# Decode attention on one core: output projections with every fourth column of wo stationary, stored four neighbours to a partition

## The chip, the core and the metric

The kernel runs on one core of a Trainium2 chip. The metric is the device time of one execution in microseconds (us), the median of several runs; lower is better. One execution was also recorded by the hardware profiler; all views of the profile come from that one, and their times count from the first instruction of its span.

The engines go by the profile's names: PE is TensorE's matmul, PEld its load of the stationary operand (LDWEIGHTS), DVE is VectorE, ACT ScalarE, POOL GpSimd, SP SyncE. A name with a q (SPq, ACTq) is the sequencer that issues DMAs. L349 is line 349 of the kernel.

## The reference

Two attention blocks, A and B, each for one new token: a query projection, 32 heads of 128 against a cache of 16384 positions (B uses only the last 4096), a softmax, the weighted sum of V, and an output projection with `wo` of 4096 x 512. The two rows of 512 are put side by side.

```python
q = (x @ wq).reshape(B, Sq, Hq, Dh).transpose(0, 2, 1, 3)
scores = jnp.einsum("bhqd,bhkd->bhqk", q, k) * (Dh ** -0.5)
p = softmax(scores, axis=-1)
o = jnp.einsum("bhqk,bhkd->bhqd", p, v)
return o.transpose(0, 2, 1, 3).reshape(B, Sq, Hq * Dh) @ wo      # a, and b with k, v cut to the window
...
return jnp.concatenate([a, b], axis=-1)                           # (1, 1, 1024) bfloat16
```

## The kernel before

All of the K and V that is needed, 336 MB, passes through SBUF once. A step of A takes two heads, a step of B eight, in two halves `u`; there are 20 steps, and their order (`steps`) is written out, with B at steps 0, 7, 13 and 19. The kernel runs under a manual schedule: each engine does its instructions in the order in which the code issues them.

For each half, VectorE multiplies K by the query (`scores_prod`, L194), adds up in a tree (`scores_tree`, L201 and L207), and ScalarE does the exponentials. TensorE then forms the weighted sums of V (`pv`, L279), with 8 or 16 rows of probabilities stationary and V moving. `evict` and `columns` (L295, L310, L314) turn the sums into columns of `s.O`, 128 dims on the partitions, one column for each head. The L310 matmuls are in f32, with 128 columns of 8 or 16 rows stationary.

Loads of K, V, wq and wo are all issued from SP's queue. x is loaded, and A's output stored, from ACT's queue. The rings `kring` and `vring` have two slots each. A's wo takes half of the last K slot, and B's last V the other half; B's wo takes a V slot when the last `pv` has read it, in five pieces (`wo_pieces`, 16, 8, 4, 2 and 2 of the 32 rows of a partition).

The last step is B's. Its two halves don't go through `pv`, but through `pv_columns` (L321): 128 pairs of a weight load of V (128 x 128 bf16) and a matmul with 4 moving columns, which give columns of O at once. The tail, in the order of the code and so of TensorE:

- the last `pv` of A, then `pv_columns` of B's first half, and A's `columns`;
- for A: `permute_o` (a transpose L331, a copy L333, four matmuls L336, a cast L340) gives `s.Op`, whose partition p and column r belong to row 32p + r of wo; `project_out_columns` (L349); `store_out`;
- `pv_columns` of B's second half, then `permute_o`, `project_out_columns` and `store_out` for B.

`project_out_columns` makes the 512 outputs as four columns of 128. For each column `c`, it goes through the rows r of wo that a partition holds, with 128 neighbouring columns of wo stationary and one column of `s.Op` moving, 128 pairs in all for A. B does so for each of its five pieces, each into four columns of its own in PSUM, since the pieces land one after the other; these are added up at the end.

`store_out` copies the four columns to SBUF (for A on ScalarE, L365; for B the sum over the pieces on VectorE, L361), in f32. Output f = 128c + p then lies on partition p in column c. A transpose on TensorE (L367) makes four rows of 128 of it, a cast to bf16 (L374 or L371) brings them back to SBUF, and a DMA stores four rows of 256 bytes (L375 from ACT's queue, L372 from SP's). The tiles `cols` and `rows` have one buffer each, which A and B share.

Of the kernel before, what the change touches and what calls it, by code (L numbers as in the profile page):

```python
# [9 lines left out]
F32 = mybir.dt.float32  # L10
BF16 = mybir.dt.bfloat16
P = 128
ACT = mybir.ActivationFunctionType
ALU = mybir.AluOpType
AX = mybir.AxisListType
# [10 lines left out]
def kernel(  # L26
# [14 lines left out]
    nc = tc.nc  # L41
# [4 lines left out]
    DN = A_wo.shape[1]  # L46
# [8 lines left out]
    one = ctx.enter_context(tc.tile_pool(name="one", bufs=1))  # L55
    ps_t = ctx.enter_context(tc.tile_pool(name="ps_t", bufs=2, space=bass.MemoryType.PSUM))
# [10 lines left out]
    identf = singles.tile([P, P], F32, tag="identf")  # L67
# [5 lines left out]
    A, B = _Side(), _Side()  # L73
# [267 lines left out]

    def project_out_columns(s, pieces):
        nf, npc = DN // P, len(pieces)
        ps = ps_s.tile([P, npc, nf], F32, tag="sp", name="out_cols")
        r0 = 0
        for k, n in enumerate(pieces):
            for c in range(nf):
                for r in range(r0, r0 + n):
                    nc.tensor.matmul(  # L349
                        ps[:, k, c : c + 1], lhsT=s.wo_t[:, r, c * P : (c + 1) * P], rhs=s.Op[:, r : r + 1],  # L350
                        start=(r == r0), stop=(r == r0 + n - 1),
                    )
            r0 += n
        s.out_ps = ps

    def store_out(s):
        nf = DN // P
        f0 = 0 if s is A else DN
        cols = one.tile([P, nf], F32, tag="cols", name="cols")
        if s is B:  # L360
            nc.vector.tensor_reduce(  # L361
                out=cols[:, :], in_=s.out_ps[:, :, :].rearrange("p k c -> p c k"), axis=AX.X, op=ALU.add
            )
        else:
            nc.scalar.copy(cols[:, :], s.out_ps[:, 0, :])  # L365
        pr = ps_t.tile([nf, P], F32, tag="tp", name="out_rows")
        nc.tensor.transpose(pr[:, :], cols[:, :], identf[:, :])  # L367
        rows = one.tile([nf, P], BF16, tag="rows", name="rows")
        dst = out[0, 0, f0 : f0 + DN].rearrange("(c f) -> c f", c=nf)
        if s is B:  # L370
            nc.vector.tensor_copy(rows[:, :], pr[:, :])  # L371
            nc.sync.dma_start(out=dst, in_=rows[:, :])  # L372
        else:
            nc.scalar.copy(rows[:, :], pr[:, :])  # L374
            nc.scalar.dma_start(out=dst, in_=rows[:, :])  # L375

    wo_pieces = (16, 8, 4, 2, 2)
    with tc.manual_schedule():
# [65 lines left out]
        columns()  # L444
        permute_o(A)
        project_out_columns(A, (HQ,))
        store_out(A)
        pv_columns(NT - 1, 1)
        permute_o(B)
        project_out_columns(B, wo_pieces)  # L450
        store_out(B)


# [28 lines left out]
```

## Time and profile before

| | us |
|---|---|
| median of 3 runs (829.58 to 830.49) | 830.06 |
| the profiled execution | 829.86 |
| its span, first to last instruction | 828.1 |
| VectorE busy (92% of the span) | 761.4 |
| TensorE busy, matmul (47%) | 387.3 |
| L201, the tree, 160 instructions | 344.9 |
| L194, the product for A, 32 instructions | 277.5 |
| L349, 256 pairs, in two bursts: from 808.43 for 3.72 us and from 819.80, in two parts, to 824.71 | 7.3 of weight loads |
| end of VectorE's last step on K (L207) | 791.39 |
| bytes read from HBM | 352.32 MB, 425 GB/s |

The page of a profile gives the busy time of each engine, then a chain: from the last instruction it is followed back to what released it, or to the instruction before it on its engine. "issue" in it is time in which an engine waited for nothing that the profile shows. A group's line gives engine, line, operation, output and input, and counts; a weight load shows in PEld, and the matmul that uses it in PE. The end of a matmul is modelled, and matmuls are pipelined, so that the distance between starts says more than the duration.

A line of the timeline has the start in us, the length, the engine, the line, the operation and the tiles; in brackets what its engine waited for before. The windows view gives for a stretch the busy time and number of instructions of each engine, the share of its full clock that TensorE was granted, and what the DMA engines did.

### The profile page before, as it was taken

Reading aid. Unit: us, or ns where it says so; the run is one execution under the profiler, and the core shown is the slowest. Engines: PE = TensorE matmul, PEld = TensorE weight load, DVE = VectorE, ACT = ScalarE, POOL = GpSimd, SP = SyncE. Lnnn points to the kernel's source line nnn. Section 1 sums busy time; section 2 is a strip of 40 time slices with the busy share of each in tenths; the row PEclk is TensorE's granted clock in tenths of the full one; section 3 lists DMA queues with packets and bytes.
Section 4 is the critical chain, followed back from the end, with each engine's and each line's share of the span. In section 5 each row is a group of like instructions: output and inputs, shape, how many; then the busy total and the mean of one; then the engine's idle time right before and its main releaser. Section 6 shows DMA issues by size and latency. Waiting matters only on the chain.

```text
span 828.1 us, 4994 instructions
## 1 busy us (share of the span) xinstructions
PE 387.3 (47%) x2100; PEld 171.3 (21%) x2100; DVE 761.4 (92%) x357; ACT 67.2 (8%) x195; POOL 0.7 (0%) x6
## 2 busy tenths in 40 slices
PE   3505061807173544637080826445362718081776
PEld 1201020303031212213030302122121203030335
DVE  1899999999999999999999999999999999999920
ACT  0111010101000001101010000011010101010110
POOL 0000000000000000000000000000000000000000
PEclk9766576859585868677685859586767767585975
DMA  9999999999999999999999999999999999999995
GB/s 380 431 431 431 428 453 423 449 416 436 431 427 431 431 440 423 439 423 455 412 450 416 452 412 432 442 423 445 419 443 418 441 421 444 424 432 432 430 430 240
DMA packets 10694, 352.64 MB, mean 426 GB/s; under 512 B 1456, under 2 KB 1456, under 8 KB 1840
## 3 DMA queue, kind: packets, MB, share of 16 engines
q1 hardware_dynamic: 10376, 352.33, 98.8%
q8 instruction: 16, 0.26, 0.1%
q10 hardware_dynamic: 296, 0.00, 0.0%
q14 instruction: 6, 0.05, 0.0%
HBM read 352.32 MB, written 0.00 MB: 425 GB/s over the span
## 4 chain that ended last, share of the span: by engine, by line
DVE 80%; DMA 15%; PE 3%; issue 1%; SPq 0%; ACT 0%; DVEq 0%
DVE kt L201 36%; DVE kt L194 36%; DMA kt<-in_A_k_cache_dram 10%; DVE sc L207 5%; DMA kt<-in_B_k_cache_dram 5%; PE o L279 1%; PE out_cols L349 1%; DVE m L212 1%; PE ocol L321 1%; DVE Mr L223 1%; DVE M L219 1%; DVE r L267 0%; SPq L135 0%; PE oc L310 0%; PE out_rows L367 0%
## 5 line engine op out<-in xcount | busy, mean ns | idle before, releaser
L201 DVE TENSOR_TENSOR kt<-kt 128x8192 bf16<-128x8192 bf16 (+3 forms) x160 | 344.9, 2156 | 4.7
L279 PE MATMUL o<-vt,pm 128*8 128x512 bf16 (+1 forms) x1216 | 306.7, 419 | 1.2 <-DMA vt<-in_A_v_cache_dram 1.2
L194 DVE TENSOR_TENSOR kt<-kt,qA 128x16384 bf16<-128x16384 bf16 x32 | 277.5, 8673 | 3.1 <-DMA kt<-in_A_k_cache_dram 3.1
L279 PEld LDWEIGHTS <-pm 128*8 128x8 bf16 (+1 forms) x1216 | 112.8, 94 | 185.4 <-issue 60.6
L214 PE MATMUL sm<-identf,m 128*1 128x128 f32 x24 | 8.5, 354 | 206.6 <-DVE m L212 206.6
L226 PE MATMUL sm<-one_f,Mr 1*128 1x1 f32 x48 | 13.3, 345 | 177.9 <-DVE Mr L223 177.9
L194 DVE TENSOR_TENSOR kt<-kt,qB 128x16384 bf16<-128x16384 bf16 x8 | 69.5, 8685 | 4.7 <-DMA kt<-in_B_k_cache_dram 4.7
L207 DVE TENSOR_REDUCE sc<-kt 128x128 f32<-128x1024 bf16 x40 | 48.8, 1220 | 2.9
L226 PEld LDWEIGHTS sm<-one_f,Mr 1*128 1x128 f32 x48 | 11.3, 291 | 184.8 <-DVE Mr L223 184.8
L214 PEld LDWEIGHTS sm<-identf,m 128*1 128x1 f32 x24 | 1.9, 79 | 209.6 <-issue 200.8
L231 ACT ACTIVATE bias<-sm 128x1 f32<-128x1 f32 x24 | 4.1, 171 | 399.5 <-PE sm L226 399.5
L295 ACT ACTIVATE o<-o,r 8x512 f32<-8x512 f32 (+1 forms) x22 | 14.9, 679 | 163.6 <-PE o L279 163.6
L310 PE MATMUL oc<-identf,o 8*128 8x2 f32 (+1 forms) x176 | 23.1, 249 | 2.4 <-ACT o L295 2.4
L310 PEld LDWEIGHTS oc<-identf,o 8*128 8x128 f32 (+1 forms) x176 | 21.2, 186 | 10.0 <-issue 6.5
L172 PE MATMUL qp<-wqt,scratch 128*128 128x512 bf16 x32 | 9.9, 486 | 13.5 <-DMA wqt<-in_B_wq_dram 13.5
L242 ACT ACTIVATE pm<-p,maskA 128x256 bf16<-128x256 bf16 x32 | 14.5, 501 | 0.5
L325 DVE TENSOR_TENSOR OB<-ocol,r 128x4 bf16<-128x4 f32 x2 | 0.3, 164 | 15.2 <-PE ocol L321 15.2
L172 PE MATMUL qp<-wqt,xbA 128*128 128x512 bf16 x32 | 8.7, 440 | 9.6 <-DMA wqt<-in_A_wq_dram 9.6
L314 ACT CAST OA<-oc 128x2 bf16<-128x2 f32 x16 | 2.6, 160 | 114.1 <-PE oc L310 114.1
L234 ACT ACTIVATE p<-sc,bias 128x256 bf16<-128x256 f32 (+1 forms) x24 | 11.3, 472 | 0.8
L242 ACT ACTIVATE pm<-p,maskB 128x128 bf16<-128x128 bf16 x32 | 10.2, 390 | 0.3
L257 PE MATMUL sm<-cs,rowsA 128*8 128x1 f32 x32 | 3.1, 167 | 14.3 <-ACT p L234 14.3
(59 smaller groups left out, 86.5 us busy)
## 6 DMA issues: line engine op xcount, KB each, us to landing
vt<-in_A_v_cache_dram SPq DMA_DIRECT2D x32, 4096.0 KB, 27.3
kt<-in_B_k_cache_dram SPq DMA_DIRECT2D x8, 4096.0 KB, 30.9
vt<-in_B_v_cache_dram SPq DMA_DIRECT2D x7, 4096.0 KB, 31.0
wqt<-in_B_wq_dram SPq DMA_DIRECT2D x1, 4096.0 KB, 12.8
wqt<-in_A_wq_dram SPq DMA_DIRECT2D x1, 4096.0 KB, 31.0
wot<-in_A_wo_dram SPq DMA_DIRECT2D x1, 4096.0 KB, 30.2
wot<-in_B_v_cache_dram SPq DMA_DIRECT2D x1, 4096.0 KB, 31.1
wot<-in_B_wo_dram SPq DMA_DIRECT2D x1, 2048.0 KB, 14.3
```

Of the source, the lines that this page charges most:

```text
L172: nc.tensor.matmul(qp[:, :, :], lhsT=s.xb[:, j, c, :], rhs=wq[:, c, j, g : g + 4, :], start=(k == 0), stop=(k == n - 1),)
L194: nc.vector.tensor_tensor(out=k, in0=k, in1=s.q[:, j : j + 1, :].broadcast_to([P, CH, DH]), op=ALU.mult)
L201: nc.vector.tensor_tensor(out=k[:, :, 0:w], in0=k[:, :, 0:w], in1=k[:, :, w : 2 * w], op=ALU.add)
L207: nc.vector.tensor_reduce(out=un.sc[:, c0 : c0 + CH], in_=k[:, :, 0:8], axis=AX.X, op=ALU.add)
L212: nc.vector.tensor_reduce(out=m[:, :], in_=un.sc[:, 0 : un.n], axis=AX.X, op=ALU.max)
L214: nc.tensor.transpose(un.sm[0:1, 0:P], m[:, :], identf[:, :])
L226: nc.tensor.matmul(un.sm[:, 128:129], lhsT=Mr[:, :], rhs=one_f[:, :], start=True, stop=True)
L234: nc.scalar.activation(out=p[:, 0 : un.n], in_=un.sc[:, 0 : un.n], func=ACT.Exp, scale=inv, bias=bias[:, :], accum_out=cs[:, :],)
L242: nc.scalar.activation(out=un.pm[:, :, j, :], in_=p[:, 0 : un.n].rearrange("p (i c) -> p i c", c=4), func=ACT.Copy, scale=s.mask[:, j : j ...
L279: nc.tensor.matmul(un.o[0 : un.rows, :], lhsT=un.pm[:, i0 + i, :, :].rearrange("p a b -> p (a b)"), rhs=V[T, u][:, 4 * i : 4 * i + 4, :], ...
L295: nc.scalar.activation(out=un.osb[0 : un.rows, :], in_=un.o[0 : un.rows, :], func=ACT.Copy, scale=un.r[0 : un.rows, 0:1],)
L310: nc.tensor.matmul(oc[:, 0 : s.nh], lhsT=un.osb[0:n, j * P : (j + 1) * P], rhs=sel[:, j, :], start=(j == 0), stop=(j == 3),)
```

## The change

In `project_out_columns` the stationary operand for column `c` is no longer the 128 neighbouring columns 128c to 128c + 127 of wo, but the columns c, c + 4, c + 8 and so on: 128 columns with a step of four elements. Column c of the result then holds, on partition p, output f = 4p + c, so that each partition has four neighbouring outputs.

In `store_out` the four columns are written to SBUF as bf16, and stored from there: 128 partitions with 4 elements, 8 bytes, each. The transpose (L367) and the second copy (L374, L371) are gone, and so is the tile `rows`. B's sum over the pieces stays on VectorE and A's copy on ScalarE; the stores stay on SP's and ACT's queues.

```diff
     def project_out_columns(s, pieces):
         nf, npc = DN // P, len(pieces)
+        wo = s.wo_t.rearrange("p r (m c) -> p r c m", c=nf)
...
                     nc.tensor.matmul(
-                        ps[:, k, c : c + 1], lhsT=s.wo_t[:, r, c * P : (c + 1) * P], rhs=s.Op[:, r : r + 1],
+                        ps[:, k, c : c + 1], lhsT=wo[:, r, c, :], rhs=s.Op[:, r : r + 1],
                         start=(r == r0), stop=(r == r0 + n - 1),
                     )
...
     def store_out(s):
         nf = DN // P
         f0 = 0 if s is A else DN
-        cols = one.tile([P, nf], F32, tag="cols", name="cols")
+        cols = one.tile([P, nf], BF16, tag="cols", name="cols")
+        dst = out[0, 0, f0 : f0 + DN].rearrange("(m c) -> m c", c=nf)
         if s is B:
-            nc.vector.tensor_reduce(
-                out=cols[:, :], in_=s.out_ps[:, :, :].rearrange("p k c -> p c k"), axis=AX.X, op=ALU.add
-            )
+            with nc.allow_low_precision("the output's own dtype"):
+                nc.vector.tensor_reduce(
+                    out=cols[:, :], in_=s.out_ps[:, :, :].rearrange("p k c -> p c k"), axis=AX.X, op=ALU.add
+                )
+            nc.sync.dma_start(out=dst, in_=cols[:, :])
         else:
             nc.scalar.copy(cols[:, :], s.out_ps[:, 0, :])
-        pr = ps_t.tile([nf, P], F32, tag="tp", name="out_rows")
-        nc.tensor.transpose(pr[:, :], cols[:, :], identf[:, :])
-        rows = one.tile([nf, P], BF16, tag="rows", name="rows")
-        dst = out[0, 0, f0 : f0 + DN].rearrange("(c f) -> c f", c=nf)
-        if s is B:
-            nc.vector.tensor_copy(rows[:, :], pr[:, :])
-            nc.sync.dma_start(out=dst, in_=rows[:, :])
-        else:
-            nc.scalar.copy(rows[:, :], pr[:, :])
-            nc.scalar.dma_start(out=dst, in_=rows[:, :])
+            nc.scalar.dma_start(out=dst, in_=cols[:, :])
```

## The prediction

> **What bounds the kernel now.** I read the head of the page, the chain that ended last, the tail's timeline, then the busy time by stretches and the DMA packets. The page first:
>
> ```profile
> span 828.1 us, 4994 instructions
> ...
> q8 instruction: 16, 0.26, 0.1%
> ...
> DVE 80%; DMA 15%; PE 3%; issue 1%; SPq 0%; ACT 0%; DVEq 0%
> ```
>
> The score products and trees on VectorE, and the K loads that feed them, fill the chain up to 791.39. The change touches none of that. It acts only in the last 20 us, where the chain (start, us, what) runs on TensorE:
>
> ```profile
> 808.43 1.15 PE out_cols L349 x38
> 809.61 2.55 PE out_cols L349 x90
> 812.77 0.96 PE ocol L321 x37
> 813.74 2.07 issue
> 815.81 2.58 PE ocol L321 x91
> 819.80 0.99 PE out_cols L349 x32
> 820.80 1.21 issue
> 822.01 2.71 PE out_cols L349 x96
> ```
>
> Two things stand here. A projection is 128 pairs of a weight load and a one-column matmul, at 2.71/96 to 1.15/38, that is 28 to 30 ns a pair with the step into the array; the starts of successive loads in the records lie 26.7 ns apart. And there are two holes, 2.07 and 1.21 us, in the midst of unbroken loops, for which no semaphore is answerable. The stretches between their ends (us, then busy and count of PE, PEld, DVE, ACT and POOL, granted clock, DMA share, GB/s) tell what they are:
>
> ```profile
> 809.60:815.81 6.21, 3.87 (x128) 3.66 (x128) 0.00 (x0) 0.42 (x2) 0.00 (x0) 0.50 0.98 412
> 815.81:822.01 6.20, 4.12 (x129) 3.87 (x129) 0.16 (x1) 0.44 (x2) 0.00 (x0) 0.50 0.64 251
> 822.01:824.81 2.80, 2.69 (x96) 2.61 (x95) 0.00 (x1) 0.00 (x0) 0.00 (x0) 0.50 0.02 6
> ```
>
> Each holds 128 loads and 128 matmuls, 256 instructions (one at a border counts in both), and lasts 6.2 us. The instruction queue's 16 packets have 16,384 bytes each, 64 for each of 256; its packets in the tail start at 813.30, 819.44 and 823.47. So TensorE's instructions come in blocks of 256; crossing into one block lets the next be fetched, and beside the full DMA load that takes 6.2 us. [...]
>
> The end, and the weight loads by kind (start, us, engine, line, what):
>
> ```profile
> 806.02 0.96 PEld L310 LDWEIGHTS oc<-identf,o 8*128 8x128 f32 x8
> ...
> 808.43 3.63 PEld L349 LDWEIGHTS <-wot 128*128 128x128 bf16 x127 [0.24 <-issue]
> ...
> 824.81 0.18 DVE L361 TENSOR_REDUCE cols<-out_cols 128x4 f32<-128x20 f32 x1 [6.23 <-PE out_cols L349]
> 825.04 0.08 PEld L367 LDWEIGHTS out_rows<-identf,cols 128*4 128x4 f32 x1 [0.42 <-DVE cols L361]
> 825.04 0.37 PE L367 MATMUL out_rows<-identf,cols 128*4 128x128 f32 x1 [0.34 <-DVE cols L361]
> 825.51 0.28 DVE L371 CAST rows<-out_rows 4x128 bf16<-4x128 f32 x1 [0.52 <-PE out_rows L367]
> 825.81 0.35 SPq L372 DMA_DIRECT2D out_dram<-rows  x1
> ```
>
> **Removed.** For B, the transpose and the cast between the reduction's end (824.99) and the store's issue (825.81). The store follows a VectorE result by 0.02 us now (cast's end 825.79), and would do so after the reduction: issue at 825.01, **0.80 us earlier**. The reduction writes bf16 instead of f32, from the same 128x20 elements: 0.18 either way. For A, the same pair (812.40 to 813.07) goes, on PE and ACT. That is worth nothing: PE's 0.4 us there lie ahead of the fetch hole at 813.74, which would grow by as much. Without the hole it would gain 0.4. Two PE instructions less move a block's border by one pair, 0.03 us.
>
> **The strided weight loads.** 128 loads for A and 128 for B now read every fourth column: 8 bytes from one element to the next where it was 2. No row of this trace has a strided weight load. The nearest row is the same load, contiguous: 26.7 ns. The far row is L310, where 128 columns of f32 come at 111 ns from start to start (0.96 us for 8, the last one's tail included). The operands in the trace tell these forms apart: L349 and L321 read 128 bf16 columns as 4 runs of 32, L310 reads a single run of 128, and 111 is about four times 26.7. [...] Between them I take **54 ns**, the geometric middle: the four runs stay, since the load still has 128 bf16 columns, as both L321 and L349 have, but each run touches four times the bytes (256 for 64), and I let that cost a factor of two.
>
> [...]
>
> With 54, block by block. The first border comes after 38 pairs of A: 809.61 + 38 x 0.0273 = 810.65. The next block is fetched 6.20 later, 816.85; the work until there, 90 pairs of A at 0.054 (4.86) and 39 of B's L321 at 0.0267 (1.04), takes 5.90, so the fetch still ends last and only the 1.04 is passed on. From 815.81 to 819.80 PE took 3.99 for the rest of L321 and the permutation; less one pair, 3.96, plus 33 pairs of B's projection (1.78) is 5.74, still under 6.20: third border 823.05. It could come by 0.46 sooner, since the loads end at 821.5 and leave the fetch alone; I don't take that. Then 95 pairs: 5.13, and the 0.14 that lay behind the last pair (824.71 less 822.01 less 96 x 0.0267): PE ends at 828.32 instead of 824.71, **+3.6 us**. Both holes shrink; what they cover are the 90 pairs of A and 33 of B that follow a border. With that cover gone (no fetch to wait for) all 256 pairs would count, 256 x 0.0273 = 7.0.
>
> **The stores.** Each was 4 rows of 256 bytes, 4 packets of 15 to 18 ns; it becomes 128 pieces of 8 bytes, 8 on each of 16 engines. The final one now takes 1.18 us from issue (825.81) to its last landing (826.99). The shape is there in the other direction, as the x load:
>
> ```profile
> xTB<-in_B_x_dram ACTq DMA_DIRECT2D x1, 1.0 KB, 7.4
> ```
>
> Its first packet starts 1.01 after its issue (1.75 against 0.74), the store's 0.78 (826.59): +0.23. Eight packets at 18 ns add 0.14. I take **+0.4**; ends 0 and +6.2 (its 7.4 in full, most of which is 4 MB of loads between its packets, and none run at the end). SP has nothing queued behind the store but the wait for its landing (waits of SP's queue; us in all, times, longest):
>
> ```profile
> SPq L477 <- DMA out_dram<-rows: 0.8, 1, 0.8
> ```
>
> A new order comes with it: `cols` is one buffer, and B's reduction may write it only when A's store has read it (before, that fell on `rows`). A's store, issued at some 812.4, or 816 with slow loads, could take the 17.2 us of the second x load while loads run; but these end at 821.5, after which nothing is between its packets. So it is read by about 822, before B's reduction at 824.8 or later: cost 0, at most 5 if it ran to 829.6. Its 128 small packets cost the loads 8 x 18 ns per engine. ACT has nothing to do behind its issue until 818.96.
>
> **Sum.** The profiled execution took 829.86 (span 828.1 and 1.76 around it), 0.20 under the median of 830.06. 829.86 - 0.80 + 3.61 + 0.40 = 833.07; on the median's scale **833.3**. With 42 ns a pair it is 831.7, with 75 it is 837.9 (there work passes fetch: 811.45, 819.24, 825.68, PE ends at 832.95). That is the likeliest case's own range.
>
> **Rivals.** (1) *The stride is free*, not slower: loads stay at 26.7, the only things left are -0.80, +0.40 and -0.03: 829.4, on the median 829.6. For it: the four runs of 32 columns stay. Against: each column now comes from its own 8 bytes. It decides below 30 ns a pair, where 133 pairs (38 + 95) cost less than the 0.4 gained. (2) *The fast form is lost*: 111 ns. 808.43 plus 38 pairs and the step gives 812.81; 90 x 0.111 + 1.04 gives 823.84; 3.96 + 33 x 0.111 gives 831.47; 95 x 0.111 + 0.14 gives 842.16, +17.45: **847.1**. For it: L310's row; against: f32 has twice the bytes and its own form. (3) *The store* with 128 pieces lands late: free loads and +6.2 instead of +0.4, 835.4; against it, an empty queue at the end. (4) The change not doing what it says would show as unchanged loads and a transpose left over; the diff leaves neither.
>
> **How the numbers follow.** Likeliest (42 to 75 ns) 0.52, (1) 0.25, (2) with all over 75 ns 0.17, (3) 0.03, a gain that my sum doesn't hold 0.03. About 0.2%, 1.66 us, is what a measurement tells from no change here: (1) is the same, at most 0.8 us can be gained, so faster has the 0.03 alone; slower 0.52 + 0.17 + 0.03 = 0.72. The range from 829.2 to 840 takes in (1), the likeliest, (3) and the nearer end of (2), some 0.82.
>
> **What would show it.** Starts of L349's loads 54 ns apart (26.7: rival 1; 111: rival 2), PE's last pair ending near 828.3 on the span's clock; holes under 0.5 us where 2.07 and 1.21 were; the last store issued 0.02 us after the reduction ends, its packets 8 per engine, its last landing some 1.6 us after issue. I am wrong if the loads don't change, or if B's reduction waits for A's store.

## The result, and the profile after

| | before | after |
|---|---|---|
| median of 14 runs each (us) | 830.09 (829.58 to 830.49) | 831.69 (831.24 to 832.10) |
| span of the profiled execution | 828.1 | 829.5 |
| start to start of two weight loads in a projection (ns, clock 0.50) | 26.7 | 33.3 |
| the last store's issue, on the span's clock | 825.81 | 825.68 |
| from that issue to its last landing | 1.18 | 2.69 |
| from that landing to the end of the span | 1.09 | 1.09 |

The changed kernel takes 1.0019 times as long, 95% interval 1.0012 to 1.0027: 1.6 us slower. The interval excludes a ratio of 1, but 1.60 lies just under the 0.2%, 1.66 us, that the prediction named as the least that a measurement tells from no change. By that measure the two kernels count as the same. The last three rows divide the 1.4 us between the two spans: the store is issued 0.13 earlier, and lands 1.5 later behind its issue.

The chain that ended last, of the changed kernel (start, us, what; steps of under 0.4 us are left out); line 349 is now 350:

```profile
806.79 1.81 PE oc L310 x8
810.00 4.40 PE out_cols L350 x128
814.40 1.02 PE ocol L321 x38
815.42 1.56 issue
816.98 2.55 PE ocol L321 x90
820.95 4.45 PE out_cols L350 x128
```

The first hole has moved by one pair, from behind the 37th of L321 to behind the 38th, as two TensorE instructions fewer ahead of it would have it. It has shrunk from 2.07 to 1.56. The second, 1.21 before, is now one step of 76 ns between two loads after the 33rd pair of B's projection. A's projection takes 4.40 us where it took 3.72, and B's 4.45.

The loads of that line, the stretches of unbroken pairs in A's and in B's projection (us, busy and count of PE, PEld, and so on; granted clock, DMA share, GB/s), and the tail's end (timeline):

```profile
L350 PEld LDWEIGHTS <-wot x256: 111/118/123, 809.7 to 825.2; 128*128 128x128 bf16 x128
```

```profile
810.01:814.24 4.23, 4.23 (x128) 4.23 (x128) 0.00 (x0) 0.00 (x0) 0.00 (x0) 0.50 0.97 413
822.08:825.21 3.13, 3.13 (x97) 3.13 (x96) 0.00 (x0) 0.00 (x0) 0.00 (x0) 0.50 0.02 5
```

```profile
825.48 0.18 DVE L364 TENSOR_REDUCE cols<-out_cols 128x4 bf16<-128x20 f32 x1 [5.75 <-PE out_cols L350]
825.68 0.35 SPq L367 DMA_DIRECT2D out_dram<-cols  x1
```

A single load takes 118 ns where it took 104 (minimum, median and maximum stand there); it overlaps its neighbours, so the 33.3 from start to start (4.23 us for 127 steps) is the price. The store is issued 0.02 us behind the reduction: the transpose and the cast are out of the path. The view of DMA issues (KB each, us from issue to landing) has what took their place:

```profile
out_dram<-cols ACTq DMA_DIRECT2D x1, 1.0 KB, 6.2
out_dram<-cols SPq DMA_DIRECT2D x1, 1.0 KB, 2.7
```

A's, beside the loads, landed at 820.79, 4.7 us before B's reduction. B's store, with the queues empty, landed in 16 shares, one after the other from 826.93 to 828.37, though the last of its packets started at 826.72. Before, four shares landed from 826.94 to 826.99.

Before and after can't be laid over each other in time. A's projection starts 1.57 us later in this profile (810.00 for 808.43), and not because of the change, which acts only from there on: the granted clock fell from 1.00 to 0.50 at 805.6 here, and at 807.9 in the profile of before, so that L310's eight pairs, for one, took 1.81 instead of 0.99. Durations and holes can be compared between profiles where the clock is the same, and totals only between medians.

### The profile page after: what moved, and what is told of

The parts are those of the page before. It is cut to its first block, busy times and chain, and to the rows that moved or that the text cites. A ratio compares the mean times of both kernels' runs of the same rounds, so it can differ in the third digit from the quotient of the medians.

```text
span 829.5 us, 4987 instructions
## 1 busy us (share of the span) xinstructions
PE 390.5 (47%) x2098; PEld 173.6 (21%) x2098; DVE 760.9 (92%) x356; ACT 66.9 (8%) x194; POOL 0.7 (0%) x6
## 4 chain that ended last, share of the span: by engine, by line
DVE 82%; DMA 12%; PE 4%; issue 1%; ACT 0%; DVEq 0%; ACTq 0%
DVE kt L201 37%; DVE kt L194 37%; DMA kt<-in_A_k_cache_dram 10%; DVE sc L207 5%; DMA xTA<-in_A_x_dram 3%; PE o L279 1%; PE out_cols L350 1%; DVE m L212 1%; PE ocol L321 1%; DVE Mr L223 1%; DVE M L219 1%; PE oc L310 0%; DVE r L267 0%; PE oT L331 0%; PE sm L226 0%
## 5 line engine op out<-in xcount | busy, mean ns | idle before, releaser
L279 PE MATMUL o<-vt,pm 128*8 128x512 bf16 (+1 forms) x1216 | 309.1, 421 | 0.5 <-DMA vt<-in_A_v_cache_dram 0.5
L279 PEld LDWEIGHTS <-pm 128*8 128x8 bf16 (+1 forms) x1216 | 113.2, 94 | 186.7 <-issue 63.3
L310 PE MATMUL oc<-identf,o 8*128 8x2 f32 (+1 forms) x176 | 23.9, 254 | 2.4 <-ACT o L295 2.4
L310 PEld LDWEIGHTS oc<-identf,o 8*128 8x128 f32 (+1 forms) x176 | 22.0, 192 | 10.0 <-issue 6.5
```

What stands on the lines that cost most here:

```text
L279: nc.tensor.matmul(un.o[0 : un.rows, :], lhsT=un.pm[:, i0 + i, :, :].rearrange("p a b -> p (a b)"), rhs=V[T, u][:, 4 * i : 4 * i + 4, :], ...
L310: nc.tensor.matmul(oc[:, 0 : s.nh], lhsT=un.osb[0:n, j * P : (j + 1) * P], rhs=sel[:, j, :], start=(j == 0), stop=(j == 3),)
```

## The experiments

### Loads and store, each alone

`e1_loads_alone` has the strided loads, and the transpose and stores of before:

```diff
         nf, npc = DN // P, len(pieces)
+        wo = s.wo_t.rearrange("p r (m c) -> p r c m", c=nf)
...
-                        ps[:, k, c : c + 1], lhsT=s.wo_t[:, r, c * P : (c + 1) * P], rhs=s.Op[:, r : r + 1],
+                        ps[:, k, c : c + 1], lhsT=wo[:, r, c, :], rhs=s.Op[:, r : r + 1],
```

> The strided loads of the change with the transpose and the four-row stores of before (so the outputs of each half stand in another order). Theory (two prices: the loads cost 33.4 instead of 26.7 ns a pair, and the 8-byte store lands 1.5 us later, against 0.8 us saved): 256 x 6.7 ns = 1.7 us of slower loads, of which the wait for instructions hides about half, so +0.6 to +1.0 over before: 830.7 to 831.1. Rival, loads alone explain the result: +2.4 (1.6 measured and the 0.8 saved), 832.5. Rival, the store alone explains it: no change, 830.1.

830.78 against 830.15 before (ratio 1.0008, 0.9999 to 1.0017): +0.6, at the lower end of the theory's span, and far from 832.5. The interval still includes a ratio of 1, so this median alone doesn't show that the loads cost time. The tail's end in its timeline:

```profile
825.68 0.18 DVE L362 TENSOR_REDUCE cols<-out_cols 128x4 f32<-128x20 f32 x1 [5.77 <-PE out_cols L350]
...
826.68 0.34 SPq L373 DMA_DIRECT2D out_dram<-rows  x1
```

The same 1.00 us from the reduction's start to the store as before, and a landing 1.19 after the issue (the records: 827.87). So from the reduction on nothing differs. The reduction starts 0.87 later in this profile, of 256 x 6.7 ns = 1.7 that the loads cost in all; but this profile had a mean granted clock of 0.657 where that of before had 0.708, and A's projection began at 810.10 where it was 808.43, so the 0.87 isn't the loads' alone. What the profiles of before and after show at one clock, 0.50, is the stretch behind the last border, where nothing is left to hide in: its 95 pairs at 6.7 ns more are 0.63 us, and from the border to PE's end it is 2.69 us before (822.01 to 824.70) and 3.30 after (822.08 to 825.38).

`e2_store_alone` is the other half: contiguous loads, `store_out` of the change.

> The contiguous loads of before with the stores of the change (outputs in another order). Theory of two prices: 0.8 saved, 1.5 lost, +0.7: 830.8; last landing 2.6 to 2.8 us after the issue. Rival, loads alone: -0.8, 829.3, landing 1.2 after the issue. Rival, store alone: +1.6, 831.7.

831.21 against 830.15 (1.0014, 1.0005 to 1.0022): +1.1. The store issues 0.02 us behind the reduction here too, and it lands later still:

```profile
out_dram<-cols SPq DMA_DIRECT2D x1, 1.0 KB, 3.2
```

0.8 saved, 2.0 lost by this profile. By the medians the two halves add up to 1.7, and the change is 1.6, so nothing else is needed. The medians don't part the halves, though: with intervals of some 0.7 us to either side, e2's +1.1 doesn't exclude the 1.6 of the rival that the store alone explains it. That both halves have a price is shown by the profiles, in the 33.3 ns between loads and in the landing.

### What the 8-byte pieces wait for

In four kernels, all with e2's contiguous loads, B's store was varied, with the same reduction in front. The two `p_pitch` kernels store the same `cols`; the two `p_runs` kernels store a zeroed tile `wide`, of which the reduction fills four columns:

```diff
+            far = dram.tile([P, 256], BF16, tag="far", name="far")      # p_pitch32: [P, 16]
-            nc.sync.dma_start(out=dst, in_=cols[:, :])
+            nc.sync.dma_start(out=far[:, 0:nf], in_=cols[:, :])
...
+            dstw = out[0, 0, f0 : f0 + DN].rearrange("(m c) -> m c", c=16)   # p_runs32; p_runs64: c=32
+            nc.sync.dma_start(out=dstw, in_=wide[0 : DN // 16, :])
```

> As e2, but B's 128 pieces of 8 bytes go to a scratch tensor in HBM with 512 bytes from one to the next (B's half of the output is not stored). Theory that pieces inside the same stretch of memory are written one behind the other: last landing 1.2 to 1.5 us after the issue. Rival, it is the number of pieces: 2.7 to 3.2 as with neighbours.

> As e2, but B's 1 KB leaves from 32 partitions with 32 bytes each (16 elements, of which 12 are zeros: not B's output). Both theories: fewer pieces in the same place, 1.3 to 1.8 us to the last landing; if the size alone decides (each piece is small against a packet), 2.7 still.

> As e2, but 16 partitions with 64 bytes each (not B's output). By the number of pieces or their neighbours 1.2 to 1.5 us; by the size alone 2.7.

> As p_pitch512, but 32 bytes from one 8-byte piece to the next (B's half of the output is not stored). With 512 bytes the last landing came 1.43 us after the issue, with 32-byte pieces side by side 1.39, with 8-byte pieces side by side 2.7 to 3.2. Theory that only pieces within the same 32 bytes wait for each other: 1.4. Rival, the stretch is 64 bytes or longer: over 1.7.

Each was run once (829.30, 830.13, 827.14 and 829.18 us), so only the landing is read from them, not the time: in the run of 827.14, p_runs64, VectorE was done with K at 789.58 where it was 791.39 before, far ahead of the store. The DMA view of p_pitch512, p_runs32 and p_pitch32, in this order:

```profile
far<-cols SPq DMA_DIRECT2D x1, 1.0 KB, 1.4
```

```profile
out_dram<-wide SPq DMA_DIRECT2D x1, 1.0 KB, 1.4
```

```profile
far<-cols SPq DMA_DIRECT2D x1, 1.0 KB, 1.4
```

To two digits more: 1.43, 1.39, 1.43, and 1.38 for p_runs64. In all four the 16 shares landed in 0.20 us, one every 13 ns. So 128 pieces cost no more than 32 or 16 when they lie 32 bytes apart or more, and 8 bytes are as quick as 64 (1.43 and 1.38 us). Only when four of them lie in the same 32 bytes do the landings spread over 1.4 to 1.9 us; the first share lands 1.25 us behind the issue there too, against 1.23 in the two `p_pitch` kernels. The number of pieces and their size are both out; that they share a place is the cause. What they wait for there the records don't show. A stretch of 32 bytes suffices to tell the cases apart; 16 was not tried, and no kernel put neighbouring pieces into the scratch tensor, though p_runs32 shows that the output tensor itself is not slow.

### What a step costs in a weight load

`q_2_8` and `q_64_6` read with other steps in A's and B's projection:

```diff
+        wo = s.wo_t.rearrange("p r f -> p (r f)")
+        step = 2 if s is A else 8                          # q_64_6: 64 and 6
...
+                    at = min(r * DN, (r0 + n) * DN - P * step) + c
...
+                        ps[:, k, c : c + 1], lhsT=wo[:, at : at + (P - 1) * step + 1 : step], rhs=s.Op[:, r : r + 1],
```

> The changed kernel with other steps between the stationary columns (so other, meaningless outputs): 2 elements (4 bytes) in A's projection, 8 (16 bytes) in B's; 4 cost 33.4 ns a pair. Theory that the load pays for each further stretch of 16 bytes or so that it opens: A 26.7 to 30, B 45 to 60. Rival, any step but 1 costs the same: 33.4 in both.

> The changed kernel with steps of 64 elements (128 bytes) in A's projection and 6 (12 bytes) in B's (other, meaningless outputs). Steps 1, 2, 4 and 8 gave 26.7, 26.7, 33.3 and 60.2 ns a pair. Theory of 16-byte stretches: at 8 each column already has its own, so 64 costs the same 60; 6 opens 24 or 25 stretches in a run of 32, against 16 at step 4 and 32 at step 8: between, some 45 to 48. Rival, the price goes on with the step: 64 far over 60.

Both were run once, and what is read from them is the distance between loads. The stretches of unbroken pairs, A's then B's, in the form of the windows above. For q_2_8:

```profile
809.52:811.92 2.40, 2.40 (x90) 2.40 (x89) 0.00 (x0) 0.00 (x0) 0.00 (x0) 0.50 0.94 403
823.01:828.82 5.81, 5.81 (x95) 5.74 (x94) 0.00 (x0) 0.00 (x0) 0.00 (x0) 0.50 0.01 3
```

and for q_64_6:

```profile
810.21:821.40 11.19, 11.19 (x127) 11.19 (x127) 0.00 (x0) 0.00 (x0) 0.00 (x0) 0.50 0.83 342
826.50:832.60 6.10, 6.09 (x128) 6.00 (x127) 0.00 (x0) 0.00 (x0) 0.00 (x0) 0.50 0.01 3
```

| step, elements | 1 | 2 | 4 | 6 | 8 | 64 |
|---|---|---|---|---|---|---|
| 16-byte stretches that a run of 32 columns opens | 4 | 8 | 16 | 24 or 25 | 32 | 32 |
| ns from load to load | 26.7 | 26.7 | 33.3 | 46.7 | 60.2 | 88.8 |

The operands in the trace show four runs of 32 in all of them, so the form that the prediction called fast was kept. All rows are at a granted clock of 0.50. The 16 bytes are an assumption of the theory, by which the row of stretches counts. From 16 to 32 such stretches the price rises by 26.9 ns for 16, 1.7 ns each; 24 would give 46.8 and 25 give 48.4, and 46.7 was measured. With 8 stretches (step 2) the same line gives 20, less than the 26.7 that were measured at steps 1 and 2. Step 64 does not fit: by stretches alone it should cost 60, and it took 89, with single steps between 74 and 101. A price that grows with the step, the rival, does not fit either: at 64 it would be some 440 by the rise from 4 to 8. Step 64 ran beside 342 GB/s of DMA; but step 4 cost 33.3 beside 413 GB/s and without, and within step 64's own stretch the mean stays at 88 to 91 while the DMA share falls from 0.99 to 0.34. So the DMA is no explanation. That stays open, and so does whether the stretch is 16 bytes: up to step 8 a cost that runs smoothly with the step fits these rows as well.

### The holes, and where the price is paid

To see whether the holes are waits for blocks of instructions, idle pairs were put early into the kernel of before, where TensorE has nothing to do:

```diff
         project_q(A)
+        pad = ps_t.tile([P, 1], F32, tag="tp", name="pad")
+        for k in range(74):                                # e_pad51: 51
+            nc.tensor.matmul(pad[:, :], lhsT=ident[:, :], rhs=ident[:, 0:1], start=True, stop=True)
         new_k(1)
```

> The kernel before with 51 idle pairs of load and matmul (102 instructions, 1.4 us of TensorE) early in the kernel, behind project_q, where TensorE has nothing to do for tens of us. Theory that the holes in the tail are waits for blocks of 256 instructions: all borders move 102 instructions forward, the first falls on the start of the last step's L321, and a fourth one falls into B's projection: PE ends about 1.5 us later, 831.6; each hole lies 51 pairs earlier in the code. Rival, the holes are waits for data (B's V, B's wo): nothing moves, 830.1.

> The same with 74 idle pairs (148 instructions). Theory of blocks: borders fall at about pair 105 of the first L321, pair 94 of A's projection, pair 93 of the second L321 and pair 88 of B's projection; the end comes 0.4 to 0.8 us earlier than before, 829.3 to 829.7. Rival, waits for data: 830.1.

829.19 with 51 (ratio 0.9990, 0.9981 to 0.9999) and 829.00 with 74 (0.9985, 0.9976 to 0.9994). Work was added, and both came out faster, by less than 0.2% but with intervals that exclude a ratio of 1, for 51 only just. In the profiles PE ends at 823.85 and 823.07, where it was 824.70. The chain of e_pad74:

```profile
807.99 2.60 PE out_cols L349 x92
811.03 1.11 PE out_cols L349 x36
812.75 2.40 PE ocol L321 x91
815.16 1.80 issue
816.96 1.14 PE ocol L321 x37
819.51 3.57 PE out_cols L349 x128
```

and of e_pad51:

```profile
809.90 3.57 PE out_cols L349 x128
814.08 3.02 PE ocol L321 x114
817.10 1.26 issue
820.30 3.57 PE out_cols L349 x128
```

The holes stand where the count of 256 puts them: behind pair 92 of A and 91 of L321 (forecast 94 and 93) with 74 pairs more, behind pair 114 of L321 with 51. Waits for data would not have moved. So the holes are the blocks. The packets say the same: in every profile of this case where TensorE stood still at a border, it went on 1.3 to 1.6 us after the end of an instruction packet (before: packets end at 814.32 and 820.52, PE goes on at 815.81 and 822.01). The gain forecast for 74, 0.4 to 0.8, was measured as 1.15. The time that I forecast for 51 was wrong by 2.4 us, even in sign. It had a border at the start of the first L321 burst release the next block only 6.2 us later; but the block's packet started at 801.28, and L321 at 803.14: so the block was on its way, while the slow L279 pairs ran (0.43 us each in the profile of before), 1.86 us before TensorE came to the border. And the last border, in B's projection, fell when the queues were empty, with its block's packet at 819.98, in time. The borders' places follow from the count, their prices don't.

`a_only` makes the change for A, and leaves B as before:

```diff
-                        ps[:, k, c : c + 1], lhsT=s.wo_t[:, r, c * P : (c + 1) * P], rhs=s.Op[:, r : r + 1],
+                        ps[:, k, c : c + 1], lhsT=wo[:, r, c, :] if s is A else s.wo_t[:, r, c * P : (c + 1) * P], rhs=s.Op[:, r : r + 1],
...
+        if s is A:
+            colsA = one.tile([P, nf], BF16, tag="colsA", name="colsA")
+            nc.scalar.copy(colsA[:, :], s.out_ps[:, 0, :])
+            nc.scalar.dma_start(out=out[0, 0, f0 : f0 + DN].rearrange("(m c) -> m c", c=nf), in_=colsA[:, :])
+            return
```

> The change for A alone: strided loads and the 8-byte store in A's projection, B as before. Theory: of A's 128 slower loads only the 38 ahead of the block border reach the end (38 x 6.7 ns = 0.25 us), the rest goes into the hole that follows; A's store lands long before the end: 830.1 to 830.5, its last landing by 821. Rival, A's 128 small pieces hold up the loads or the instruction blocks that share the queues: 830.8 or more, and a release of the second L321 hole over 6.5 us behind the border before.

829.82 against 830.04 (0.9998, 0.9989 to 1.0007): nothing to be told, not even the 0.25 us of the 38 pairs ahead of the border. In this profile a wait of 0.25 us at that border followed them anyway. A's 128 loads at 33.3 ns, and its store of 128 pieces, are covered by the holes and by the time until B's end. Neither sign of the rival came: it is 829.82 and not 830.8, and the second L321 went on 5.9 us behind its border, not over 6.5. The store had landed at 820.56, as forecast. As far as this interval tells, all of the change's price is B's.

> The changed kernel with the 74 idle pairs of e_pad74. Theory: now 92 of A's pairs lie ahead of the border (0.6 us passed on) and all of B's 128 behind the last hole (0.86), and the store costs its 0.7 to 1.1: 2.2 to 2.6 over e_pad74's 829.0, 831.2 to 831.6, about where the changed kernel is without them. Rival, the borders don't matter for the loads' price: 1.6 over e_pad74, 830.6.

831.03 against 830.04 (1.0014, 1.0005 to 1.0023). Against e_pad74 that is 1.0014/0.9985 = 1.0029, 2.4 us, as the theory had it; but the two intervals together leave some 1.3 to 3.5, so the rival's 1.6 is not excluded. Nor did it come about as I had said. The first hole's end did not move (817.03 against 816.96): in e_pad74 A's 92 pairs are followed by a wait of 0.44 us (810.59 to 811.03 in its chain), and the slower loads went mostly into that. Instead a step of 0.8 us appeared behind pair 87 of B's projection, where e_pad74 had none; the instruction packet ahead of it took 1.86 us instead of 1.03, for a reason that the records don't show. Inconclusive as a test of the theory. As a version, e_pad74 was the fastest of those that compute the reference, 1.15 us below the kernel before; the idle pairs are a way of shifting borders, and a change of the program anywhere ahead of the tail shifts them again.

## Why the prediction held, and where it did not

The direction was right, 833.3 was 1.6 too high, and 831.69 lies in the range. It is also what the sum gives for 42 ns a pair, the edge of the likeliest case, but that is luck: at 33.3 ns the loads lie outside that case's 42 to 75 and outside the first rival's 30, and two terms were mis-sized in opposite directions, the loads by 3 us too much and the store by some 1.1 to 1.6 too little. With 33.3 ns and nothing else changed the sum would have given about 830.5. By the prediction's own least difference, 1.66 us, the 1.60 is on the side of no change.

- *The strided loads, 54 ns a pair.* The mechanism held: each load is dearer (33.3 ns for 26.7), the four runs of 32 stay, and the wait for blocks hides a share (A's, in a_only). The price was 33.3. The geometric middle between 26.7 and 111 rested on no row for a step; the 111 belonged to another form and was never near. It was also read at another clock: L310's 111 ns stand at a granted clock of 1.00, the 26.7 at 0.50. At 0.50 L310 takes some 214 (profile of after), eight times 26.7 and not four, while the bf16 loads of L321 take 25 at 1.00 and 27 at 0.50. The geometric middle at one clock would have been some 76, further off still. With 33.3 my own steps give 809.61 + 38 x 0.0067 + 12.40 + 95 x 0.0333 + 0.14 = 825.57 for PE's end. The profile has 825.4, but by other steps: A's projection began 1.57 us later, and the last two blocks came 5.7 and 5.1 us behind their borders instead of 6.2 each, 1.6 less together. The path lost about 0.6 (by e1's median, and by the 95 pairs behind the last border) and not 3.6. The first hole stayed at 1.56, where I had both under 0.5.
- *The store, +0.4.* The 128 packets came as forecast, of 8 bytes, at 7 to 9 ns each where I took 18. But I priced only what is sent, and the cost lies in the landing: +1.5 in the changed kernel, +2.0 in e2, because four pieces share 32 bytes. This was in the sum the term with the wrong cause. The third rival had a late landing, but for 6.2 us and for another reason, packets between packets of loads.
- *0.80 saved* behind B's reduction: 0.80 measured (1.00 us from the reduction's start to the issue before, 0.20 after).
- *A's transpose and cast worth nothing, A's loads covered, A's store no hindrance:* shown by a_only, for the three together and within its interval of some 0.7 us to either side. B's reduction did not wait for A's store, which had landed at 820.8, 4.7 us ahead.
- *The holes are blocks of 256 instructions:* shown by the holes' places in the changed kernel, in e1 (which keeps the transposes, and its hole behind the 37th pair) and in the two with idle pairs. That each takes 6.2 us was too firm: from a border to the next at which TensorE had to wait it was 5.1 (after) to 7.3 us (q_2_8), and in e_pad74 a block was there after 4.9 without a wait. What sets this is not shown.
- *The first rival,* free loads and 829.6, failed on both its terms: 33.3 lies over its 30 ns, and the store's +0.4 was too little.

## What to carry to other kernels

Before a transpose in front of a store is traded for a direct store, see how the bytes fall in memory: here 8-byte pieces, four in each 32 bytes, landed one behind the other over 1.4 to 1.9 us, where pieces 32 bytes apart took 0.20, and the store lost 1.5 to 2.0 us for the 0.80 that the transpose and its cast had cost. In a stationary operand a step of two bf16 elements cost nothing here (26.7 ns from load to load, as at step 1), a step of four a quarter more (33.3), of six 46.7, of eight 60.2 and of 64 88.8, all at a granted clock of 0.50; for other steps the price has to be measured. And where TensorE runs through small matmuls without a break, look for holes every 256 instructions (2.07 and 1.21 us in the kernel before): work between a border and the hole behind it was free as long as the hole lasted (A's slower loads: 829.82 us in a_only against 830.04), and work behind the last one counted in full (95 pairs: 3.30 us where they took 2.69).

## What was not expected

Adding 1.4 to 2 us of idle matmuls early made the kernel about 1 us faster (829.19 and 829.00 for 830.15), by shifting where the instruction blocks end. 128 writes of 8 bytes land as quickly as 16 of 64 (1.43 and 1.38 us) where they lie 32 bytes apart or more. And a step of 64 elements costs a weight load 89 ns, with a scatter of 74 to 101, where steps up to 8 are steady within 2 ns, block borders apart, once the loop has run for some ten loads.
